# Pooled v of the early pairs by TensorE products, later loads and later product places for the first late pairs

## The chip, the cores and the metric

The kernel runs on one core of one Trainium2 chip. The metric is device time in microseconds, from the runs of the whole program; lower is better. The kernel before takes 948.91 us, the median of three runs (948.26 to 949.22).

## What is computed

A batch of 8 goes through attention and a mixing feed-forward. The attention has two parts: one over sequences pooled by four (a mean of four neighbours of q, k and v), repeated back to full length, and one local part in which each position sees the three neighbours on each side. Their sum x goes into a low-rank mix over positions and a two-layer FFN.

```
B, H, S, D = 8, 8, 576, 64
q_d, k_d, v_d = mean over groups of 4 positions          # 144 positions
out_up    = repeat(softmax(q_d k_d^T / 8) v_d, 4)
out_local = softmax(mask(|i - j| < 4, q k^T / 8)) v
x = out_up + out_local, heads side by side               # 576 x 512 per batch
u = x + (x^T U V)^T                                      # rank 32
out = u + relu(u W1) W2                                  # 512 -> 2048 -> 512
```

## The kernel before, in words

The work is 32 **pairs** of heads, four to a batch, numbered 0 to 31 here. Pairs 0 to 4 (`NE = 5`) take the early path, all others the late path. The early path ends quickly, since TensorE (PE) has nothing else to do until the four pairs of the first batch are finished; the late path gives the local part to GpSimd (POOL) and VectorE (DVE) through DRAM, beside the FFN.

The **FFN** runs per half batch of 288 positions in 16 steps: `ffn1` takes 12 products (L908: high and low parts of u and W1) into a PSUM bank `ps_h`, ScalarE (ACT) makes `hH` from it by ReLU, DVE `hL`, and three steps later `ffn2` takes 12 products (L931) into four accumulators. The 16 blocks of W1 and 16 of W2 are loaded once, as raw 32-bit halves into three shared buffers (`w1r`, `w2r`), and converted (`convert`, L355): ACT makes `upper` (L358), DVE `c` (L361), ACT the high part (L365), and DVE or POOL the low part (L369; DVE for the first eight W1 blocks).

An **early pair** has two strands. `early_global` (L442) pools q and k on POOL (`smq`, `smk`), multiplies them on PE into two banks `ps_s` (L455), takes the row maxima (DVE), the exponentials `E_e` (ACT), transposes them (`ps_t`, L488, copied back by ACT, L491) and multiplies them with the pooled v, `vs_e` (`ps_a`, L500). That `vs_e` is made by POOL in two sums (L459, L461) from `vre`, a load of v of its own (`load_vr`, L591). `local_blocks` (L611) makes scores of 32 positions against 38 keys (`ps_b`, L607), their exponentials `ms_b`, transposes (`ps_bt`, L647) and the products with the windows of v, `vw` (`ps_ba`, L659). `vw` has two buffers that the pairs take in turn (`vw_115` for pairs 0, 2 and 4, `vw_116` for 1 and 3), as have `vs_e` and `E_e`. Both strands meet in `early_mix` (L668: `ps_hu`, `ps_u`), which writes u as `uH` (ACT, L710) and `uL` (DVE).

A **late pair** loads `gq`, `gT` and two `vr`, pools on POOL, multiplies into `ps_b` (L735 and L742, one block of products), copies the local scores out to DRAM (ACT `se`, L760; `s_s`), takes exponentials `E` (L539), transposes (`ps_t`, L553), copies back (L557) and multiplies (`ps_a`, L566).

**The order** of all instructions is set ahead of time by a planner (`Plan.run`, L112). It plays the five engines with assumed durations; on each engine, of the operations that are ready, the one with the smallest priority number is next. Pair p has priorities 10p to 10p + 2, the FFN fills (from 1000 up). So pairs 5 and 6 have 50 to 72. A `margin` (L102) delays the time at which an operation counts as ready: 0.5 us for PE operations of priority 50 to 999 that depend on another engine. A load may not begin in the plan before `at`, 25 us for priorities from 35 up (L276). All loads are issued by SyncE (SP), which keeps its order and stops at a load whose buffer isn't free. PSUM for `ps_s` of pair p and `ps_b` of pair p + 1 is the same two banks.

Of the kernel before, what the change touches and what calls it, by code (L numbers as in the profile page):

```python
# [11 lines left out]
F32 = mybir.dt.float32  # L12
# [58 lines left out]
class Plan:  # L71
# [147 lines left out]
def attn_mix_ffn_kernel(ctx: ExitStack, tc, q, kp, vl_in, qT, kT, v, U, Ub, V, w1, w2_in, mask, band, eye, pool, vw, ident, outT):  # L219
# [221 lines left out]

    def early_global(b, hp, prio, qt, kt, vr):  # L442
        sq = work(True, glo, [128, SD], F32, "smq")
# [8 lines left out]
        def s_mm():  # L452
# [5 lines left out]
        vs = ring([4, D], "vs_e")  # L458
        pool_tt(512, lambda: nc.gpsimd.tensor_tensor(  # L459
            out=vr()[:, :, 0:2 * D], in0=vr()[:, :, 0:2 * D], in1=vr()[:, :, 2 * D:4 * D], op=ALU.add), [vr], [vr], prio, 2.2)  # L460
        pool_tt(256, lambda: nc.gpsimd.tensor_tensor(  # L461
            out=vs()[:QH], in0=vr()[:, :, 0:D], in1=vr()[:, :, D:2 * D], op=ALU.add), [vr], [vs], prio, 2.2)
        E = ring([4, SD], "E_e")
# [18 lines left out]
        for hh in range(2):  # L482
            pt = psum(ps_m, "ps_t", "m:g", 2)

            def t_mm(hh=hh, pt=pt):
                for c in range(2):
                    for a in range(2):
                        nc.tensor.transpose(view(pt, SD)[:, c, a * QH:(a + 1) * QH],  # L488
                                            E()[:QH, 2 * hh + a, c * QH:(c + 1) * QH], ident_sb[:QH, :QH])
            op(PE, 0.44, t_mm, [(E, hh), "ident"], [pt], prio)  # L490
            act(288, lambda hh=hh, pt=pt: nc.scalar.activation(E()[:QH, 2 * hh:2 * hh + 2], view(pt, SD), AF.Copy),  # L491
                [pt], [(E, hh)], prio, 0.12)
        pa = psum(ps_m, "ps_a", "m:g", 2)
        out = lambda: pa()[:QH, :4 * D].rearrange("p (a h d) -> p a h d", a=2, h=2)

        def a_mm():
            for hh in range(2):
                for a in range(2):
                    for c in range(2):
                        nc.tensor.matmul(out()[:, a, hh, :], E()[:, 2 * hh + c, a * QH:(a + 1) * QH],  # L500
                                         vs()[:, 2 * hh + c, :], start=(c == 0), stop=(c == 1))
        op(PE, 1.2, a_mm, ek + [vs], [pa], prio)
        od = work(True, glo, [QH, 2, 2, D], F32, "od")
# [87 lines left out]
    def load_vr(b, h0, prio):  # L591
        t = buf(early_pool, [QH, 4, 4 * D], F32, "vre", None, 2)
        dma(lambda: nc.sync.dma_start(out=t().rearrange("p (h a) x -> p h a x", h=2), in_=v[b, h0:h0 + 2].rearrange(
            "h (a p r) d -> p h a (r d)", a=2, r=4)), [], [t], prio, 480)
        return t

# [359 lines left out]
    def attention(b, pairs=range(HP)):  # L956
        for hp in pairs:
            p = 10.0 * (b * HP + hp)
            if b * HP + hp < NE:
# [104 lines left out]
```

## Time and profile before

One profiled execution took 949.7 us; its span, from the first instruction to the last, is 947.9 us.

| | us |
|---|---|
| median of the runs | 948.91 |
| profiled execution | 949.7 |
| its span | 947.9 |
| first FFN product begins | 65.47 |
| last PE product ends | 943.7 |

A profile row of an engine reads: start, duration, engine, line, operation, output <- inputs, shape, count, and in brackets the idle time ahead of it with what ended it. The row of a group has busy time and mean duration behind the first bar, and the idle time ahead of its members behind the second. Windows give, for a stretch of time, the busy time of every engine, the clock granted to TensorE and the share of the DMA engines' time. A product of floats shows as two records.

### The profile page before, as it was taken

To read this page: it belongs to the slowest core of one execution; us is meant where nothing else is said; L and a number is where in the kernel's file an instruction comes from. 1 tells how busy PE (TensorE), PEld (TensorE's weight loads), DVE (VectorE), ACT (ScalarE), POOL (GpSimd) and SP (SyncE) were. 2 spreads that over 40 slices of the span, in tenths; PEclk is the share of its full clock that TensorE was granted. 3 is DMA by queue.
4 is the path that set the end of the run, shared out by engine and by line. 5 is a ranking of instruction groups with operands and counts; after the bars stand their busy time and mean duration, and the time that the engine had idled before them with its cause. 6 is when DMAs were issued, how large, how long until landed. Compare 5 with 4: busy or idle time off the path is not lost.

```text
span 947.9 us, 26576 instructions
## 1 busy us (share of the span) xinstructions
PE 921.7 (97%) x10805; PEld 903.6 (95%) x10805; DVE 473.9 (50%) x958; ACT 383.8 (40%) x1221; POOL 524.0 (55%) x563
## 2 busy tenths in 40 slices
PE   5799899999999999999999999999999999999998
PEld 4678899999999999999999999999999999999998
DVE  4784755545645444565555555444565544322212
ACT  4687744434443344443344344443443343121111
POOL 5655776675666564775758747565655546021010
PEclk9899899999999999999999999999999999999999
DMA  9977555564454545544565455456444442200000
GB/s 274 300 241 257 170 137 149 132 152 115 127 131 115 123 103 147 138 107 124 138 155 133 119 132 136 109 132 155 115 128 125 120 90 58 64 1 26 6 21 26
DMA packets 215977, 119.19 MB, mean 126 GB/s; under 512 B 168132, under 2 KB 192304, under 8 KB 215856
## 3 DMA queue, kind: packets, MB, share of 16 engines
q1 hardware_dynamic: 215856, 117.51, 48.3%
q8 instruction: 85, 1.39, 0.6%
q14 instruction: 36, 0.29, 0.1%
HBM read 87.37 MB, written 30.09 MB: 124 GB/s over the span
## 4 chain that ended last, share of the span: by engine, by line
PE 87%; DMA 5%; DVE 3%; ACT 3%; issue 1%; SPq 1%; DVEq 0%; ACTq 0%
PE acc L931 38%; PE ps_h L908 37%; PE ps_a L566 3%; PE ps_b L735 2%; PE ps_hu L864 2%; PE ps_t L553 1%; PE ps_b L742 1%; DMA w2r<-in_W 1%; DVE c L361 1%; DMA w1r<-in_W 1%; ACT upper L358 1%; PE ps_u L879 1%; DMA gT<-in_kT 1%; DMA ur<-in_Ub 1%; DMA ur<-in_U 1%
## 5 line engine op out<-in xcount | busy, mean ns | idle before, releaser
L815 POOL TENSOR_TENSOR Pt<-vl,at 128x896 f32<-128x896 f32 (+1 forms) x135 | 219.1, 1689 | 143.3 <-DVE at L798 74.7
L908 PE MATMUL ps_h<-uH,W1H 128*128 128x288 f32 x1024 | 295.0, 288 | 1.0 <-DVE hL L916 0.7
L908 PE MATMUL ps_h<-uL,W1H 128*128 128x288 f32 x1024 | 293.2, 286 | 0.0
L908 PE MATMUL ps_h<-uH,W1L 128*128 128x288 f32 x1024 | 293.0, 286 | 0.0
L916 DVE SCALAR_TENSOR_TENSOR hL<-ps_h,hH 128x288 fp32r<-128x288 f32 x256 | 116.6, 455 | 334.7 <-ACT hH L915 334.3
L915 ACT ACTIVATE hH<-ps_h 128x288 fp32r<-128x288 f32 x256 | 104.7, 409 | 372.4 <-PE ps_h L908 371.4
L931 PE MATMUL acc<-hH,W2a 128*128 128x288 f32 x1024 | 218.7, 292 | 0.0
L908 PEld LDWEIGHTS ps_h<-uH,W1H 128*128 128x128 f32 x1024 | 193.9, 189 | 2.0 <-DVE hL L916 1.0
L908 PEld LDWEIGHTS ps_h<-uL,W1H 128*128 128x128 f32 x1024 | 193.8, 189 | 0.0
L908 PEld LDWEIGHTS ps_h<-uH,W1L 128*128 128x128 f32 x1024 | 193.8, 189 | 0.0
L931 PEld LDWEIGHTS acc<-hH,W2a 128*128 128x128 f32 x1024 | 171.2, 191 | 0.4
L931 PE MATMUL acc<-hL,W2a 128*128 128x288 f32 x512 | 147.6, 288 | 0.0
L820 DVE TENSOR_REDUCE acc<-Pt 128x128 f32<-128x1024 f32 (+1 forms) x135 | 145.3, 1105 | 4.0 <-ACT Pt L809 2.8
L931 PE MATMUL acc<-hH,W2c 128*128 128x288 f32 x512 | 109.9, 291 | 0.0
L931 PE MATMUL acc<-hH,W2b 128*128 128x288 f32 x512 | 106.9, 288 | 0.0
L931 PEld LDWEIGHTS acc<-hL,W2a 128*128 128x128 f32 x512 | 97.9, 191 | 0.0
L856 POOL TENSOR_TENSOR xL<-xL,xH 116x640 fp32r<-116x640 f32 x27 | 41.8, 1547 | 90.1 <-ACT xH L855 83.0
L931 PEld LDWEIGHTS acc<-hH,W2c 128*128 128x128 f32 x512 | 85.2, 189 | 0.3
L931 PEld LDWEIGHTS acc<-hH,W2b 128*128 128x128 f32 x512 | 84.5, 189 | 0.1
L931 PE MATMUL acc<-hL,W2b 128*128 128x288 f32 x256 | 73.2, 286 | 0.0
L931 PE MATMUL acc<-hL,W2c 128*128 128x288 f32 x256 | 73.2, 286 | 0.0
L941 POOL TENSOR_TENSOR o<-uH,uL 128x288 f32<-128x288 f32 x48 | 37.0, 795 | 49.0 <-DMA out_t<-o 43.8
(141 smaller groups left out, 1286.6 us busy)
## 6 DMA issues: line engine op xcount, KB each, us to landing
vl<-in_vl SPq DMA_DIRECT2D x27, 480.0 KB
w1r<-in_W SPq DMA_DIRECT2D x16, 511.8 KB
w2r<-in_W SPq DMA_DIRECT2D x16, 511.8 KB
gT<-in_kT SPq DMA_DIRECT2D x27, 291.0 KB
gq<-in_qT SPq DMA_DIRECT2D x27, 288.0 KB
vr<-in_v SPq DMA_DIRECT2D x54, 144.0 KB
up_s<-od SPq DMA_DIRECT2D x108, 72.0 KB
ul<-up_s SPq DMA_DIRECT2D x27, 288.0 KB
```

Source lines behind the costliest of these rows:

```text
L358: act(n, lambda: nc.scalar.activation(c()[:pp, :n].bitcast(F16).rearrange("p (n two) -> p n two", two=2)[:, :, 1], raw()[:pp, :2 * n].bitc ...
L566: nc.tensor.matmul(out()[:, 2 * hh + a, :], Es[hh]()[:, c, a * QH:(a + 1) * QH], vss[hh]()[:, c, :], start=(c == 0), stop=(c == 1))
L735: nc.tensor.matmul(ps[hh]()[c * QL:(c + 1) * QL, r * KL:(r + 1) * KL], qr()[o, n * QL:(n + 1) * QL], kr()[o, n * QL:n * QL + KL], start=Tr ...
L815: nc.gpsimd.tensor_tensor(out=Pt()[:, :n, :, 0:7].rearrange("p s d o -> p o s d"), in0=win, in1=at()[:, ps, :].rearrange("p s o -> p o s") ...
L820: dve(8.5 * n * D, lambda n=n, ps=ps, Pt=Pt: nc.vector.tensor_reduce(out=acc()[:, ps, :], in_=Pt()[:, :n], axis=AX.X, op=ALU.add), [(Pt, 0 ...
L856: pool_tt(640, lambda: nc.gpsimd.tensor_tensor(out=xL(), in0=xL().bitcast(F32), in1=xH().bitcast(F32), op=ALU.subtract), [xL, xH], [xL], prio)
L864: nc.tensor.matmul(pv(), Ust[:, j, :], xx()[:, :, j, :], start=(i == 0 and j == 0), stop=(i == 1 and j == MJ - 1))
L908: nc.tensor.matmul(ps()[:, :TN], w[:, dc, fs], turns(u()[:, dc, :]), start=(n == 0), stop=(n == 3 * NDC - 1))
L915: last_h[i] = act(TN, lambda: nc.scalar.activation(hH(), ps()[:, :TN], AF.Relu), [ps], [hH], FIRST, 0.05)
L916: dve(TN, lambda: nc.vector.scalar_tensor_tensor(hL(), ps()[:, :TN], 0.0, hH().bitcast(F32), op0=ALU.max, op1=ALU.subtract), [ps, hH], [hL ...
L931: nc.tensor.matmul(ac[e]()[:, :TN], w2(fc, w)[:, es], turns(hx()), start=(fc == 0 and n == 0), stop=(fc == NFC - 1 and n == 2))
L941: pool_tt(TN, lambda e=e, o1=o1: nc.gpsimd.tensor_tensor(out=o1()[:, :TN].bitcast(F32), in0=uH()[:, e, :].bitcast(F32), in1=uL()[:, e, :]. ...
```

## The change

The pooled v of pairs 0 to 4 comes from `vw` instead of a load of its own: its windows start three positions ahead of each block of 32, and a stripe matrix of zeros and ones, appended to `pool_sb` (144 to 200 columns), adds up four rows at a time. 18 blocks times two heads are 36 products per pair, written into free columns of the two `ps_s` banks, and four DVE copies take them to `vs_e`. The load of `vre` and both POOL sums go. Since the sums lie now as 128 + 16 pooled positions instead of 72 + 72, the transposes of E are cut as 128 and 16: one copy stays on ACT (144 columns instead of 288), one of 16 rows goes to DVE.

Three settings move as well. The PE margin for priorities 49 to 69 becomes 2.0. Loads of priority 49 and up may not begin in the plan before 42 us. Low parts of W1 go to POOL from block 4 on instead of 8.

```diff
-MARGIN, MARGIN_FROM = (0.5,0.0,0.0,0.0,0.0), 50
+MARGIN, MARGIN_FROM, FIRST_MARGIN = (0.5, 0.0, 0.0, 0.0, 0.0), 50, 2.0
...
-        o.margin = MARGIN[eng] * (MARGIN_FROM <= prio < 1000 and any(d.eng != eng for d in deps))
+        o.margin = (FIRST_MARGIN if eng == PE and prio < 70 else MARGIN[eng]) * (
+            MARGIN_FROM - 1 <= prio < 1000 and any(d.eng != eng for d in deps))
...
-        return op(SP, issue, fn, r, w, prio, move=0.01 + kb / 390.0, at=AT if prio >= 35 else 0.0, lat=lat + late)
+        return op(SP, issue, fn, r, w, prio, move=0.01 + kb / 390.0, at=42 if prio >= 49 else AT if prio >= 35 else 0.0, lat=lat + late)
...
-        convert(raw, 128, CN, lambda: W1H[:, :, fs], lambda: W1L[:, :, fs], NDC, f"W1_{f}", "c1", prio, rest=DVE if f < 8 else POOL)
+        convert(raw, 128, CN, lambda: W1H[:, :, fs], lambda: W1L[:, :, fs], NDC, f"W1_{f}", "c1", prio, rest=DVE if f < 4 else POOL)
...
-        pool_tt(512, lambda: nc.gpsimd.tensor_tensor(
-            out=vr()[:, :, 0:2 * D], in0=vr()[:, :, 0:2 * D], in1=vr()[:, :, 2 * D:4 * D], op=ALU.add), [vr], [vr], prio, 2.2)
-        pool_tt(256, lambda: nc.gpsimd.tensor_tensor(
-            out=vs()[:QH], in0=vr()[:, :, 0:D], in1=vr()[:, :, D:2 * D], op=ALU.add), [vr], [vs], prio, 2.2)
+        def v_mm():
+            for c in range(4):
+                for g in range((NL - c + 3) // 4):
+                    for hh in range(2):
+                        o = slice(hh * KW, (hh + 1) * KW)
+                        nc.tensor.matmul(ps[hh]()[g % 4 * QL:(g % 4 + 1) * QL, 2 * SD + g // 4 * D:2 * SD + (g // 4 + 1) * D],
+                                         pool_sb[o, 168 - 8 * c:168 - 8 * c + QL], vw_t()[o, 4 * g + c, :],
+                                         start=(c == 0 and g < 4), stop=(c == 3))
+        op(PE, 0.9, v_mm, [vw_t, "pool"], [(p, "v") for p in ps], prio)
+        for hh in range(2):
+            for c, n in enumerate((128, QL)):
+                dve(D, lambda hh=hh, c=c, n=n: nc.vector.tensor_copy(out=vs()[:n, 2 * hh + c, :], in_=ps[hh]()[:n, 2 * SD + c * D:2 * SD + (c + 1) * D]),
+                    [(ps[hh], "v")], [(vs, hh, c)], prio)
...
-            act(288, lambda hh=hh, pt=pt: nc.scalar.activation(E()[:QH, 2 * hh:2 * hh + 2], view(pt, SD), AF.Copy),
-                [pt], [(E, hh)], prio, 0.12)
+            act(SD, lambda hh=hh, pt=pt: nc.scalar.activation(E()[:, 2 * hh], pt()[:, :SD], AF.Copy), [pt], [(E, hh)], prio, 0.12)
+            dve(SD, lambda hh=hh, pt=pt: nc.vector.tensor_copy(
+                out=E()[:SD - 128, 2 * hh + 1], in_=pt()[:SD - 128, SD:2 * SD]), [pt], [(E, hh)], prio)
...
-                od = early_global(b, hp, p, qt, kt, load_vr(b, 2 * hp, p))
+                od = early_global(b, hp, p, qt, kt, vw_t)
```

Because the planner sets the order, it moves in many places. Three of them follow; lines behind the changed ones have moved by up to 12 (L607 is now L613, L908 is L914).

The first is PE at the start of the program, from the scores of pair 0 to the first `ps_a`. In a row stand line, operation, output <- inputs, shape and count; `ps_up` pools U. Before:

```order
L607 MATMUL ps_b<-kd,qt 32x38 x36
L455 MATMUL ps_s<-smk,smq 72x144 x4
L647 MATMUL ps_bt<-ident_sb,ms_b_103 128x128 x5
L488 MATMUL ps_t<-ident_sb,E_e_111 72x72 x4
L386 MATMUL ps_up<-Ublk,pool_sb 72x64 x6
L488 MATMUL ps_t<-ident_sb,E_e_111 72x72 x4
L619 LDWEIGHTS eye_sb
L619 MATMUL ps_b<-band_sb,eye_sb 128x190
L619 LDWEIGHTS eye_sb
L619 MATMUL ps_b<-band_sb,eye_sb 128x190
L607 MATMUL ps_b<-kd,qt 32x38 x36
L500 MATMUL ps_a<-vs_e_107,E_e_111 72x64 x8
```

And now:

```order
L613 MATMUL ps_b<-kd,qt 32x38 x36
L456 MATMUL ps_s<-smk,smq 72x144 x4
L465 MATMUL ps_s<-vw_115,pool_sb 32x64 x36
L387 MATMUL ps_up<-Ublk,pool_sb 72x64 x6
L499 MATMUL ps_t<-ident_sb,E_e_111 128x72 x2
L499 MATMUL ps_t<-ident_sb,E_e_111 16x72 x2
L653 MATMUL ps_bt<-ident_sb,ms_b_103 128x128 x5
L499 MATMUL ps_t<-ident_sb,E_e_111 128x72 x2
L499 MATMUL ps_t<-ident_sb,E_e_111 16x72 x2
L456 MATMUL ps_s<-smk,smq 72x144 x4
L465 MATMUL ps_s<-vw_116,pool_sb 32x64 x36
L512 MATMUL ps_a<-vs_e_107,E_e_111 72x64 x8
```

The products of `vw` and `pool_sb` (L465) of pairs 0 and 1 stand ahead of the transposes and of `ps_a`, and the pooled scores of pair 1 have moved ahead of its local scores.

The second is ACT around the scores of pair 6 (`se`, `E`) and the conversions of the last W2 blocks and of U (`ur`, `Ust`). Before:

```order
L358 ACTIVATE upper_86<-w2r 128x512
L536 ACTIVATE nb<-mx 72x2
L358 ACTIVATE upper_87<-ur 116x160
L539 ACTIVATE E,rs<-ps_b,nb 72x144 x2
L365 ACTIVATE W2b<-c_1912 128x512
L365 ACTIVATE Ust<-cu 116x5x32
L915 ACTIVATE hH<-ps_h 128x288
L536 ACTIVATE nb<-mx 72x2
L539 ACTIVATE E,rs<-ps_b,nb 72x144 x2
```

And now:

```order
L359 ACTIVATE upper_87<-ur 116x160
L366 ACTIVATE W2b<-c_2028 128x512
L921 ACTIVATE hH<-ps_h 128x288
L366 ACTIVATE Ust<-cu 116x5x32
L766 ACTIVATE se<-ps_b 96x114
L766 ACTIVATE se<-ps_b 32x342
L766 ACTIVATE se<-ps_b 96x114
L766 ACTIVATE se<-ps_b 32x342
L548 ACTIVATE nb<-mx 72x2 x2
L551 ACTIVATE E,rs<-ps_b,nb 72x144 x3
L921 ACTIVATE hH<-ps_h 128x288
L551 ACTIVATE E,rs<-ps_b,nb 72x144
```

All conversions now stand ahead of the first copy `se` of pair 6. On PE, between pair 5's transposes and its `ps_a` there are 42 FFN products where there were 24, and between pair 6's scores and its transposes 48 where there were 72.

The third is SP, from the loads of pair 4 on (`qt`, `kd`, `vw_115`) to those of pair 5 (`gq`, `gT`, `vr`, `vl`) and the W1 blocks among them. Before:

```order
L583 DMA qt<-in_qT 128x576
L599 DMA kd<-in_kT 128x582
L583 DMA gq<-in_qT 128x576
L583 DMA gT<-in_kT 128x582
L522 DMA vr<-in_v 72x2x256
L783 DMA vl<-in_vl 128x960
L410 DMA w1r<-in_W 128x2047 x2
L588 DMA vw_115<-in_vw 128x1152
L410 DMA w1r<-in_W 128x2047
```

And now, from the `vw_116` of pair 3:

```order
L600 DMA vw_116<-in_vw 128x1152
L411 DMA w1r<-in_W 128x2047 x3
L600 DMA vw_115<-in_vw 128x1152
L411 DMA w1r<-in_W 128x2047 x3
L595 DMA gq<-in_qT 128x576
L411 DMA w1r<-in_W 128x2047
L595 DMA gT<-in_kT 128x582
L534 DMA vr<-in_v 72x2x256
L789 DMA vl<-in_vl 128x960
L411 DMA w1r<-in_W 128x2047 x3
```

Pair 5's loads have moved behind pair 4's last one. Six blocks of W1 stood ahead of its `gq` and ten behind it; now twelve stand ahead, and the last three behind `vl`.

More of the change, by code (lines that the diff above doesn't have):

```diff
@@ L323, in attn_mix_ffn_kernel @@
     eye_sb = early_pool.tile([128, 128], BF16, name="eye_sb")
-    pool_sb = early_pool.tile([128, 144], F32, name="pool_sb")
+    pool_sb = early_pool.tile([128, 200], F32, name="pool_sb")
     Ublk = early_pool.tile([128, NS, 2 * R], F32, name="Ublk")
@@ L440, in pool_halves, with early_global @@
             out=out(), in0=gh()[..., 0], in1=gh()[..., 1], op=ALU.add), [gh], [out], prio, 1.75)
-    def early_global(b, hp, prio, qt, kt, vr):
+    def early_global(b, hp, prio, qt, kt, vw_t):
         sq = work(True, glo, [128, SD], F32, "smq")
@@ L486, in t_mm @@
                 for c in range(2):
+                    n = (128, SD - 128)[c]
                     for a in range(2):
-                        nc.tensor.transpose(view(pt, SD)[:, c, a * QH:(a + 1) * QH],
-                                            E()[:QH, 2 * hh + a, c * QH:(c + 1) * QH], ident_sb[:QH, :QH])
+                        nc.tensor.transpose(pt()[:n, c * SD + a * QH:c * SD + (a + 1) * QH],
+                                            E()[:QH, 2 * hh + a, c * 128:c * 128 + n], ident_sb[:QH, :QH])
             op(PE, 0.44, t_mm, [(E, hh), "ident"], [pt], prio)
-            act(288, lambda hh=hh, pt=pt: nc.scalar.activation(E()[:QH, 2 * hh:2 * hh + 2], view(pt, SD), AF.Copy),
-                [pt], [(E, hh)], prio, 0.12)
+            act(SD, lambda hh=hh, pt=pt: nc.scalar.activation(E()[:, 2 * hh], pt()[:, :SD], AF.Copy), [pt], [(E, hh)], prio, 0.12)
+            dve(SD, lambda hh=hh, pt=pt: nc.vector.tensor_copy(
+                out=E()[:SD - 128, 2 * hh + 1], in_=pt()[:SD - 128, SD:2 * SD]), [pt], [(E, hh)], prio)
         pa = psum(ps_m, "ps_a", "m:g", 2)
@@ L501, in a_mm @@
                                          vs()[:, 2 * hh + c, :], start=(c == 0), stop=(c == 1))
-        op(PE, 1.2, a_mm, ek + [vs], [pa], prio)
+        op(PE, 1.2, a_mm, ek + [(vs, hh, c) for hh in range(2) for c in range(2)], [pa], prio)
         od = work(True, glo, [QH, 2, 2, D], F32, "od")
@@ L589, in load_vw @@
         return vw_t
[L591 to L595, printed above, removed]
     def load_kd(b, h0, prio):
@@ L1030 @@
     pool = np.arange(128)[:, None] // 4 + 64 == np.arange(144)[None, :]
+    own = np.arange(128)[:, None] % 64 - 3
+    pool = np.concatenate([pool, (own // 4 + 24 == np.arange(56)[None, :]) & (own >= 0) & (own < 32)], axis=1)
     arrays = {
```

## The prediction, made before the result was known

> **What bounds the kernel now.** Read the page's head first, then the windows, one row to a stage.
>
> ```profile
> span 947.9 us, 26576 instructions
> ...
> PE 921.7 (97%) x10805; PEld 903.6 (95%) x10805; DVE 473.9 (50%) x958; ACT 383.8 (40%) x1221; POOL 524.0 (55%) x563
> ```
> ```profile
> 0.00:20.00 20.00, 10.56 (x221) 8.40 (x221) 9.51 (x26) 8.21 (x28) 11.15 (x22) 1.00 0.91 271
> 20.00:34.00 14.00, 11.00 (x263) 8.80 (x263) 7.25 (x17) 8.71 (x33) 8.74 (x12) 0.88 0.94 290
> 34.00:65.00 31.00, 27.50 (x573) 22.58 (x573) 26.90 (x59) 25.38 (x75) 17.29 (x21) 0.94 0.85 270
> 65.00:92.00 27.00, 25.57 (x296) 23.98 (x294) 14.76 (x25) 19.81 (x48) 16.77 (x13) 1.00 0.75 238
> 92.00:125.00 33.00, 29.27 (x310) 28.32 (x309) 23.03 (x39) 19.93 (x54) 24.46 (x25) 0.90 0.61 185
> 125.00:900.00 775.00, 774.03 (x8798) 767.98 (x8797) 382.39 (x775) 296.00 (x970) 442.49 (x469) 1.00 0.47 113
> ```
>
> The columns are window, length, busy time (and instructions) of PE, PEld, DVE, ACT and POOL, then granted clock, DMA share and GB/s. From 125 us on PE idles 1 us in 775: nothing on another engine is worth anything there, and only work put on PE or taken from it counts. All that the change can win or lose lies before: PE idles 9.4, 3.0 and 3.5 us in the first three windows, 1.4 and 3.7 us in the next two. The clock falls to 0.88, 0.94 and 0.90 in three of them. Next, PE's timeline shows where; the bracket is the idle time and what ended it.
>
> ```profile
> 10.99 1.30 PE L647 MATMUL ps_bt<-ident_sb,ms_b 128*128 128x128 f32 x5 [2.79 <-DMA ident_sb<-in_ident]
> ...
> 12.81 0.57 PE L488 MATMUL ps_t<-ident_sb,E_e 72*72 72x72 f32 x3 [0.40 <-ACT E_e L473]
> 13.40 1.70 PE L386 MATMUL ps_up<-Ublk,pool_sb 128*72 128x64 f32 x12
> ...
> 20.28 0.79 PE L659 MATMUL ps_ba<-vw,et 38*32 38x64 f32 x56 [1.12 <-issue]
> ...
> 33.70 0.27 PE L607 MATMUL ps_b<-kd,qt 64*32 64x38 f32 x7 [2.68 <-issue]
> ...
> 34.44 0.85 PE L607 MATMUL ps_b<-kd,qt 64*32 64x38 f32 x72
> ...
> 41.01 1.03 PE L659 MATMUL ps_ba<-vw,et 38*32 38x64 f32 x80
> ...
> 65.47 0.39 PE L908 MATMUL ps_h<-uH,W1H 128*128 128x288 f32 x1 [0.28 <-DVE ob L663]
> ```
> ```profile
> 89.85 0.67 PE L553 MATMUL ps_t<-ident_sb,E 72*72 72x72 f32 x8
> ...
> 94.44 0.73 PE L566 MATMUL ps_a<-vs,E 72*72 72x64 f32 x8 [0.94 <-ACT E L557]
> ...
> 95.96 0.73 PE L566 MATMUL ps_a<-vs,E 72*72 72x64 f32 x8 [0.79 <-ACT E L557]
> ...
> 112.06 0.45 PE L553 MATMUL ps_t<-ident_sb,E 72*72 72x72 f32 x4 [0.46 <-ACT E L539]
> ...
> 114.05 0.69 PE L553 MATMUL ps_t<-ident_sb,E 72*72 72x72 f32 x4 [1.54 <-ACT E L539]
> ```
>
> No wait of PE ends at the pooled v, neither at its load nor at its two sums. The FFN begins at 65.47; pairs 5 and 6 then stop PE four times, 0.94 + 0.79 + 0.46 + 1.54 = 3.73 us, all on ScalarE. The clock rows behind these stops:
>
> ```profile
> 96.00:100.00 4.00, 4.00 (x24) 4.00 (x25) 3.30 (x6) 2.90 (x6) 4.00 (x5) 0.62 0.93 336
> 100.00:104.00 4.00, 4.00 (x118) 3.79 (x117) 3.16 (x5) 1.78 (x5) 2.44 (x2) 0.96 0.45 120
> ...
> 112.00:116.00 4.00, 2.39 (x14) 2.23 (x15) 2.03 (x5) 3.92 (x17) 4.00 (x4) 0.75 0.26 27
> 116.00:120.00 4.00, 4.00 (x29) 4.00 (x28) 2.92 (x5) 1.09 (x3) 4.00 (x4) 0.82 0.03 5
> ```
>
> The missing clock is 4 x (0.38 + 0.04) = 1.7 us behind the first two stops and 4 x (0.25 + 0.18) = 1.7 us behind the second two. So the stops and their clock hold 3.7 + 3.4 = 7.1 us.
>
> **The change, part by part.** *Products for the pooled v.* Five pairs get 36 products each; PE's records count a product of floats twice, so the 72 records of the scores (0.85 us) and the 80 of the local sums (1.03, or 0.93 for 72) are the like: small tiles, four column groups and two row halves in turn. I take 0.9 us, 4.5 us for five.
>
> Pair 0's stand ahead of everything that PE began at 10.99 and wait for `pool_sb`, whose landing no row shows. It was issued after `ident_sb`, which ended the wait at 10.99, and one load of 288 KB less stands ahead (1.1 us at 271 GB/s): not before 9.9. At 13.40 it was there. I take 12.0, so the queue behind starts 12.0 + 0.9 - 11.0 = 1.9 us later and loses its wait of 0.40: +1.5 us, ends -0.2 and +3.3.
>
> The other four cost 3.6 us in windows where PE idles 3.0 + 3.5 us of 45. Nothing assigns them to the gaps: I take 2.6, ends 0 and 3.6.
>
> *Removed.*
>
> ```profile
> L459 POOL TENSOR_TENSOR vre<-vre 72x512 f32<-72x512 f32 x5 | 6.3, 1265 | 8.8 <-DMA vre<-in_v 8.8
> ...
> L461 POOL TENSOR_TENSOR vs_e<-vre 72x256 f32<-72x256 f32 x5 | 3.6, 727 | 3.9 <-PE ps_a L500 3.8
> ```
> ```profile
> vre<-in_v SPq DMA_DIRECT2D x5, 288.0 KB
> ```
> ```profile
> L491 ACT ACTIVATE E_e<-ps_t 72x288 f32<-72x288 f32 x10 | 4.0, 399 | 4.0 <-PE ps_t L488 4.0
> ```
> ```profile
> L504 DVE TENSOR_TENSOR od<-ps_a,ri 72x256 f32<-72x256 f32 x5 | 2.1, 417 | 1.9 <-PE ps_a L500 1.9
> ...
> L639 DVE RECIPROCAL ri_b<-re 128x10 f32<-128x10 f32 x5 | 1.0, 206 | 0.3 <-ACT re L638 0.3
> ```
>
> POOL loses 9.9 us, the load queue 1.44 MB (5.1 us at 280 GB/s), ACT about a third of each of ten copies (1.2 us). DVE gains 20 copies of 64 columns and 10 of 144, between 206 and 417 ns each: about 0.23 and 0.29, 7.5 us in all, and loses four subtractions of W1. Its windows have 6.8 and 4.1 us idle between 20 and 65 us, so they hide, if they don't stand ahead of a score reduction; then they are in the late end below. POOL takes those four over, in time that it has gained. The loads for pair 5 also leave the queue in front of pair 4's (the third place shown in the section on the change). This relief can return at most the 6.5 us that PE idles from 20 to 65, and at least nothing, since two of these waits, 1.12 and 2.68, ended at nothing that the trace names. I take about half, -3.1 us. Up to the FFN's start: 1.5 + 2.6 - 3.1 = **+1.0 us**, bounds -6.7 and +6.9.
>
> *The later places of pairs 5 and 6.* An FFN product takes 1.47 / 12 = 0.1225 us:
>
> ```profile
> 117.63 1.47 PE ps_h L908 x12
> ```
> ```profile
> 93.07 0.77 ACT L358 ACTIVATE upper<-w2r 128x512 f16<-128x512 bf16 x1 [3.23 <-DMA w2r<-in_W]
> ...
> 95.52 0.39 ACT L557 ACTIVATE E<-ps_t 72x288 f32<-72x288 f32 x1
> ...
> 110.94 0.39 ACT L358 ACTIVATE upper<-ur 116x160 f16<-116x160 bf16 x1 [0.93 <-DMA ur<-in_U]
> ```
> ```profile
> 113.17 0.83 ACT E L539 x4
> ```
> ```profile
> 80.79 1.48 ACT L760 ACTIVATE se<-ps_b 96x114 f32<-96x114 f32 x4
> ```
>
> Pair 5's transposes ended at 90.5 and ScalarE's second copy at 95.9, behind a conversion that waited 3.23 us for W2. Between transposes and `ps_a` stood 24 FFN products (2.9 us), now 42 (5.1 us); the first half of `ps_a` takes 0.7 us more, so the second copy is needed 5.8 us after the transposes and took 5.4. Both waits and their 1.7 us of clock go: -3.4. Pair 6 waited for its exponentials behind the conversion of U (110.94). U's conversion now stands before the copies out of the scores, and no conversion stands among the exponentials. But between scores and transposes there are 48 FFN products (5.9 us) where there were 72 (8.8). Four copies (1.5 us), four exponentials (two with their sums took 0.83, so 1.7) and two scalings and a ReLU copy, none longer than the 0.39 of a copy of E (1.2), make 4.4 us and the semaphores: it just fits unless U or W2 lands late. I count a quarter of its 3.7 us as won, 0.9. Together **-4.3 us**, bounds -7.1 and +1.0.
>
> The clock gate can be weighed here: after stops of 0.94 and 0.79 us the clock reads 0.62. The Trainium skill, "TensorE: Matmul & The Clock Gate", Part 1, has the half clock come only after an idle window of about 3.4 us. By that rule stops this short would cost no clock and the gain would be 1.7 + 0.5 instead of 3.4 + 0.9, a time of 947.7; the row differs from it, and decides.
>
> *Sum.* +1.0 - 4.3 = -3.3 us. The profiled execution took 949.7 us, 1.8 above its span of 947.9; 949.7 - 3.3 = 946.4. The median of the runs is 0.8 below that execution: **945.6 us**.
>
> **Rivals.** *Weights late, slower.* Before pair 3's last `uH` ScalarE now converts 16 blocks of W1 and one of W2, where it converted 13 and wrote 12 high parts; the last three W1 loads, all ahead of `uH` now, stand right behind 1.2 MB for pair 5.
>
> ```profile
> 61.53 0.63 ACT L365 ACTIVATE W1H<-c 128x512 fp32r<-128x512 f32 x1
> ...
> 62.44 0.77 ACT L358 ACTIVATE upper<-w1r 128x512 f16<-128x512 bf16 x1
> ...
> 63.08 0.39 ACT L710 ACTIVATE uH<-ps_u 128x288 fp32r<-128x288 f32 x1
> ```
>
> Four more conversions of 0.77 and as many high parts of 0.63 are 5.6 us on an engine that keeps its order and had 5.6 us idle of 31, and 1.2 MB is 4.4 us of loading. It decides if the sixteenth W1 block lands after about 62 us, since `uH` ran at 63.08. If the FFN starts 6.5 us later, +6.5 - 4.3 = +2.2; with pair 6's gain gone too, +3.1: 951 to 952 us. For it: DVE and ACT are the fullest there (26.9 and 25.4 of 31). Against it: the loads begin earlier, with 1.44 MB less to carry.
>
> *Moved, not won, within 0.2%.* The relief is worth little, the early part costs 2 to 4 us, and only pair 5's 3.4 come back: -1.4 to +0.6, 947.5 to 949.5. For it: no wait of PE ended at the pooled v, so 4.5 us of new products buy nothing by themselves. Against it: the gaps of pair 5 have a clear cause and a clear cover.
>
> *Products that don't overlap, slower.* If the 36 products run one by one like the transposes (four in 0.45 us, row 112.06), they take 4 us a pair, 20 in all, 15.5 more than counted: 961 us. Against it: the 72 records at 34.44, laid out in the same way, take 12 ns each. The Trainium skill, "TensorE: Matmul & The Clock Gate", section "Back-to-back issue gap", has starts never closer than about 25 ns, which by that page makes 1.8 us a pair and a time of about 950; the row is below that floor.
>
> **Chances.** Forecast 0.56, moved 0.24, weights late 0.15, no overlap 0.05. A measurement of this kernel tells about 0.2% (1.9 us) from no change, so faster is below 947.0 and slower above 950.8: 0.56, 0.24, 0.20. The range takes most of the early bounds with the late gain, 941, and the late weights, 952; about 0.06 is left on either side.
>
> **What would show it.** The v products as one block of about 0.9 us a pair; the first of them ended by a load near 12 us; the FFN's first product at 65 to 68 us; no wait in front of pair 5's `ps_a`, a small one at most in front of pair 6's transposes, and a clock of 1.0 behind both; PE's busy time up by some 2 to 5 us and still no idle time after 125 us. I am wrong if the FFN starts after 70, if ScalarE stands at a W1 or U load for over 2 us with PE waiting behind it, or if PE starts to wait after 125 us because pairs 5 to 7 come too late for the second batch.

## The result, and the profile after

The changed kernel takes longer:

| | before | changed |
|---|---|---|
| median of 5 runs each, us | 948.91 | 956.07 (953.30 to 958.95) |
| ratio, 95% interval | | 1.0070 (1.0045 to 1.0095) |
| profiled execution, us (span) | 949.70 (947.9) | 956.07 (954.3) |
| first FFN product of TensorE, us | 65.47 | 73.58 |
| from there to the end of the span, us | 882.4 | 880.7 |

A later set of runs, with 23 of before, gave 956.52 and 1.0085 (1.0065 to 1.0104). The forecast was 945.6 with a range up to 952: the sign was wrong, and the time lies outside the range. The whole loss stands ahead of the FFN.

The head of the changed kernel's page and its windows, with the columns of the prediction's rows (window, length, busy time and instructions of PE, PEld, DVE, ACT, POOL, then clock, DMA share, GB/s):

```profile
span 954.3 us, 27312 instructions
...
PE 923.5 (97%) x11165; PEld 905.5 (95%) x11165; DVE 481.9 (51%) x984; ACT 385.5 (40%) x1221; POOL 521.5 (55%) x557
```
```profile
0.00:20.00 20.00, 11.13 (x349) 9.07 (x350) 10.39 (x34) 9.00 (x34) 9.37 (x22) 1.00 0.78 278
20.00:34.00 14.00, 10.34 (x212) 8.63 (x211) 8.99 (x25) 8.49 (x25) 2.18 (x4) 0.88 0.54 183
34.00:65.00 31.00, 25.25 (x809) 20.49 (x808) 22.70 (x64) 23.23 (x76) 18.38 (x17) 1.00 0.79 261
65.00:92.00 27.00, 23.48 (x271) 21.40 (x265) 14.25 (x24) 13.81 (x30) 14.27 (x13) 0.87 0.53 173
92.00:125.00 33.00, 29.08 (x323) 27.70 (x321) 21.34 (x30) 23.44 (x59) 24.03 (x20) 1.00 0.67 203
125.00:900.00 775.00, 774.05 (x8805) 768.25 (x8806) 392.36 (x786) 300.91 (x987) 450.15 (x479) 1.00 0.48 115
```

From 125 us on nothing has changed. In 92 to 125 the clock is back at 1.00 from 0.90, as forecast. In 34 to 65 PE issues 809 products where it issued 573, and idles 5.75 us where it idled 3.50. Its timeline shows what those waits are:

```profile
18.52 0.99 PE L665 MATMUL ps_ba<-vw,et 38*32 38x64 f32 x74
21.21 0.31 PE L665 MATMUL ps_ba<-vw,et 38*32 38x64 f32 x6 [1.70 <-issue]
...
23.36 0.54 PE L613 MATMUL ps_b<-kd,qt 64*32 64x38 f32 x37
26.35 0.51 PE L613 MATMUL ps_b<-kd,qt 64*32 64x38 f32 x35 [2.45 <-issue]
...
39.07 0.33 PE L653 MATMUL ps_bt<-ident_sb,ms_b 128*128 128x128 f32 x1 [1.10 <-issue]
...
49.44 0.27 PE L613 MATMUL ps_b<-kd,qt 64*32 64x38 f32 x6 [2.50 <-issue]
...
58.15 0.80 PE L465 MATMUL ps_s<-vw,pool_sb 64*32 64x64 f32 x35
59.92 0.63 PE L465 MATMUL ps_s<-vw,pool_sb 64*32 64x64 f32 x37 [0.97 <-issue]
...
65.57 0.41 PE L665 MATMUL ps_ba<-vw,et 38*32 38x64 f32 x19 [0.51 <-issue]
...
73.58 0.59 PE L914 MATMUL ps_h<-uH,W1H 128*128 128x288 f32 x1
```

Six stops "issue", that is, stops that end at nothing the trace names, sum to 9.23 us; before had two, 1.12 + 2.68 = 3.80. Most of them cut through the middle of a block of equal products (74 and 6, 37 and 35) whose operands are the same two tiles, so an operand is unlikely to be what was waited for. All other idle time ahead of the FFN is the same: 12.5 us against 12.35. PE's busy time there is 51.85 us against 49.32. So of the FFN's 8.1 us of delay, 5.4 are these stops and 2.5 busy time.

Where do they stand? The windows from 0 to just ahead of each stop count what PE had issued; the numbers behind x in the first two groups are its products and its weight loads. Changed kernel, then before:

```profile
0.00:21.20 21.20, 11.13 (x349) 9.07 (x350) 10.88 (x34) 10.20 (x37) 9.37 (x22) 1.00 0.77 269
0.00:26.34 26.34, 13.82 (x476) 11.18 (x476) 14.50 (x45) 13.16 (x45) 9.37 (x22) 1.00 0.80 283
0.00:39.06 39.06, 25.38 (x730) 20.96 (x730) 24.27 (x73) 21.79 (x73) 13.80 (x30) 0.96 0.71 248
0.00:49.43 49.43, 33.24 (x985) 27.13 (x985) 30.32 (x89) 29.46 (x96) 21.19 (x34) 0.97 0.74 251
0.00:59.91 59.91, 42.76 (x1238) 34.77 (x1239) 39.59 (x112) 36.62 (x117) 26.95 (x39) 0.97 0.73 249
0.00:65.56 65.56, 46.78 (x1366) 38.19 (x1367) 42.65 (x123) 41.07 (x132) 30.48 (x44) 0.97 0.73 247
```
```profile
0.00:20.27 20.27, 10.56 (x221) 8.40 (x221) 9.51 (x26) 8.21 (x28) 11.42 (x23) 1.00 0.91 270
0.00:33.69 33.69, 21.27 (x475) 16.95 (x476) 16.75 (x43) 16.91 (x61) 19.58 (x33) 0.95 0.92 279
```

The two counts of a row add up to 699, 952, 1460, 1970, 2477 and 2733, and 442 and 951: always 442 plus a multiple of 254, within 7 records, whatever line stands there. The queues in section 3 of the two pages, changed kernel first, say what comes in pieces of that size:

```profile
q8 instruction: 88, 1.44, 0.6%
q14 instruction: 36, 0.29, 0.1%
```
```profile
q8 instruction: 85, 1.39, 0.6%
q14 instruction: 36, 0.29, 0.1%
```

The columns are packets and MB. A packet of q8 has 16.4 KB. PE's records of a whole run, products and weight loads together, are 2 x 11165 = 22330 and 2 x 10805 = 21610: 253.8 and 254.2 for each packet of q8, while q14 has as many packets in both. In all fourteen profiles PE's records over 254 give the packets of q8 within one. So the reading is: PE's instructions come by DMA in blocks of about 254, and PE stops where it has used up a block before the next is there. In the changed kernel, PE went on after these stops at 26.35, 39.07, 49.44 and 59.92 us, each two blocks after the one before: a block every 6.4, 5.2 and 5.2 us. In 34 to 65 us its 1617 records in 31 us would need one every 4.9. During four of the six stops the DMA engines are full or nearly so (DMA share is the last but one column). In that of 1.70 us it was 0.41, and in that of 0.51 us nothing moved, so full engines are not the whole reason why a block comes late; the rest stays open.

```profile
23.90:26.30 2.40, 0.00 (x0) 0.00 (x0) 1.27 (x4) 0.80 (x2) 0.00 (x0) 1.00 0.99 318
...
38.00:39.00 1.00, 0.00 (x0) 0.00 (x0) 1.00 (x4) 0.85 (x5) 1.00 (x3) 1.00 1.03 375
...
47.00:49.40 2.40, 0.00 (x0) 0.00 (x0) 0.49 (x2) 0.79 (x2) 2.40 (x2) 1.00 0.87 284
...
59.00:60.00 1.00, 0.07 (x9) 0.07 (x13) 0.50 (x2) 0.00 (x0) 0.00 (x0) 1.00 1.11 259
```

### The profile page after: what moved, and what is told of

Read it like the earlier page. It is cut to its first block, busy times and chain, and to the rows that moved or that the text cites. A ratio compares the mean times of both kernels' runs of the same rounds, so it can differ in the third digit from the quotient of the medians.

```text
span 954.3 us, 27312 instructions
## 1 busy us (share of the span) xinstructions
PE 923.5 (97%) x11165; PEld 905.5 (95%) x11165; DVE 481.9 (51%) x984; ACT 385.5 (40%) x1221; POOL 521.5 (55%) x557
## 4 chain that ended last, share of the span: by engine, by line
PE 90%; DMA 2%; DVE 2%; ACT 2%; issue 2%; POOL 1%; SPq 0%; DVEq 0%; POOLq 0%; ACTq 0%
PE acc L937 38%; PE ps_h L914 38%; PE ps_a L578 3%; PE ps_b L741 2%; PE ps_hu L870 2%; PE ps_t L565 1%; PE ps_b L748 1%; DVE c L362 1%; PE ps_u L885 1%; POOL W1L L370 1%; DMA w2r<-in_W 1%; DMA gT<-in_kT 1%; DMA vraw<-in_V 1%; ACT upper L359 1%; PE ps_s L465 0%
## 5 line engine op out<-in xcount | busy, mean ns | idle before, releaser
L914 PE MATMUL ps_h<-uH,W1H 128*128 128x288 f32 x1024 | 296.1, 289 | 2.7 <-DVE hL L922 2.7
L914 PE MATMUL ps_h<-uL,W1H 128*128 128x288 f32 x1024 | 294.0, 287 | 0.0
L914 PE MATMUL ps_h<-uH,W1L 128*128 128x288 f32 x1024 | 294.0, 287 | 0.0
L914 PEld LDWEIGHTS ps_h<-uH,W1H 128*128 128x128 f32 x1024 | 194.7, 190 | 3.9 <-DVE hL L922 3.3
L914 PEld LDWEIGHTS ps_h<-uL,W1H 128*128 128x128 f32 x1024 | 194.6, 190 | 0.0
L914 PEld LDWEIGHTS ps_h<-uH,W1L 128*128 128x128 f32 x1024 | 194.6, 190 | 0.0
L893 POOL TENSOR_TENSOR uL<-xT,uH 128x288 fp32r<-128x288 f32 x54 | 42.0, 799 | 69.4 <-ACT uH L891 69.4
```

The costliest lines, as they stand in the source:

```text
L893: pool_tt(TN, lambda uH=uH, uL=uL, uf=uf: nc.gpsimd.tensor_tensor(out=uL()[:, hp, :], in0=uf(), in1=uH()[:, hp, :].bitcast(F32), op=ALU.su ...
L914: nc.tensor.matmul(ps()[:, :TN], w[:, dc, fs], turns(u()[:, dc, :]), start=(n == 0), stop=(n == 3 * NDC - 1))
```

## The experiments

The theory is **supply**, the blocks of instructions above. By it a product costs its records, not only its time, and loads that are taken away pay because blocks come sooner. There are two rivals. **Time**: only the products' own time on PE and the waits between engines count. **Settings**: the four numbers changed beside the v products (margin, loads from 42, W1's low parts of blocks 4 to 7 on GpSimd) cost the time. Three sets ran, each beside before; ratios are to that before, with 95% intervals. "Stops" are those put down to issue ahead of the FFN in the profiled execution.

| kernel | median us | ratio | stops, us | FFN starts |
|---|---|---|---|---|
| before (set 1 / 2 / 3) | 948.94 / 948.51 / 948.15 | | 3.80 | 65.47 |
| 1 dense products | 957.65 | 1.0077 (1.0047 to 1.0108) | 4.23 | 76.17 |
| 1 large products | 956.07 | 1.0089 (1.0056 to 1.0121) | 6.19 | 70.70 |
| 1 settings alone | 948.76 | 0.9997 (0.9975 to 1.0019) | 4.16 | 67.58 |
| 1 v change alone | 952.42 | 1.0040 (1.0021 to 1.0059) | 7.85 | 73.21 |
| 2 changed kernel again | 956.52 | 1.0085 (1.0065 to 1.0104) | 9.11 | 75.06 |
| 2 v as 6 large products | 947.74 | 0.9996 (0.9981 to 1.0011) | 0.26 | 65.27 |
| 2 v by 10 products of 36 | 946.90 | 0.9983 (0.9969 to 0.9996) | 0.20 | 66.01 |
| 2 margin of before | 955.61 | 1.0071 (1.0053 to 1.0088) | 6.37 | 73.32 |
| 3 before, small v loads | 942.60 | 0.9946 (0.9924 to 0.9968) | 0.74 | 61.79 |
| 3 loads of before | 952.61 | 1.0056 (1.0037 to 1.0076) | 8.55 | 70.45 |
| 3 W1 of before | 960.18 | 1.0135 (1.0114 to 1.0156) | 7.65 | 72.32 |
| 3 v as 12 large products | 950.86 | 1.0022 (1.0006 to 1.0037) | 0.50 | 70.58 |

**Set 1: products added to before, and the change in two halves.** Dense products, in `s_mm` of before:

```diff
                                     start=True, stop=True)
+            for n in range(18):
+                for hh, o in enumerate(heads):
+                    nc.tensor.matmul(ps[hh]()[n % 4 * QL:(n % 4 + 1) * QL, 2 * SD:2 * SD + D],
+                                     sq()[o, :QL], sk()[o, :D], start=True, stop=True)
```

> The kernel of before, in which each early pair's block of pooled score products (L455) issues 36 more products of the size of the v products (K 64, 32 rows out, 64 columns), whose results nothing reads; pooled v stays on GpSimd and every setting is that of before. The theory of instruction supply (TensorE stands, for nothing that the trace names, where it has used up a block of some 254 records before the next has come): 144 more TensorE records a pair, 720 in all, as in the change; the stops put down to issue before the FFN grow from 3.8 us to 7 to 10 us, each at a multiple of about 254 records, PE's busy time grows by 4 to 6 us, and the FFN starts 7 to 11 us later: 954 to 960 us. The rival, that only the products' own time and the waits between engines cost: the stops put down to issue stay at 3 to 5 us, the time rises by no more than the products' 4 to 6 us: 949 to 954 us.

Large products, at the same place:

```diff
+            for n in range(4):
+                for hh, o in enumerate(heads):
+                    nc.tensor.matmul(ps[hh]()[:QH, 2 * SD:3 * SD],
+                                     sq()[o, n % 2 * QH:(n % 2 + 1) * QH], sk()[o], start=True, stop=True)
```

> The kernel of before, in which each early pair's block of pooled score products issues 8 more products of its own size (72 rows out, 144 columns), unread: about the same TensorE time as the 36 small ones of the other kernel of this set (some 1 us a pair), but 32 records a pair in place of 144. The theory of instruction supply: stops put down to issue stay at 3 to 5.5 us, time 949 to 953 us, at least 3 us below the kernel with small products. The rival, that TensorE's time and the waits between engines cost: within 1.5 us of the kernel with small products.

This pair missed. The dense kernel's time came as the theory had it, the stops did not, and the large products cost nearly as much (956.07, outside the theory's 949 to 953, and within 1.6 us of the other). The groups of the added products, dense and large:

```profile
0.00:75.00 75.00, 6.32 (x360) 0.86 0.76 238
```
```profile
0.00:75.00 75.00, 7.01 (x80) 0.89 0.81 256
```

(busy time of these products alone in the first 75 us, then clock, DMA share and GB/s.) The large ones took 7.0 us and cost 7.1; the dense ones took 6.3 and cost 8.7. By these medians added PE time counts about one for one in the kernel of before, and what is left for the records is too small beside the intervals. The large kernel's median is also a poor measure: its ten runs fall apart into six of 953.1 to 956.4 us, of which the profile is one, and four of 962.0 to 964.8; by the ratios it is the dearer of the two. And by windows of 1 us up to 75 us, PE loses 9.1 us to the lower clock in the dense kernel, 8.3 in the large one and 3.4 in before. This pair decides nothing between supply and time. Nor is the sum of the stops a measure of supply: in the dense kernel PE ran at half clock from 47 to 60 us, below the pace of the blocks, and had no need to stop. Where it did stop, the grid holds: 1208, 1462, 1717 and 1973 records in the one, 442, 1206 and 1968 in the other.

The settings alone, on before:

```diff
-MARGIN, MARGIN_FROM = (0.5,0.0,0.0,0.0,0.0), 50
+MARGIN, MARGIN_FROM, FIRST_MARGIN = (0.5, 0.0, 0.0, 0.0, 0.0), 50, 2.0
...
-        return op(SP, issue, fn, r, w, prio, move=0.01 + kb / 390.0, at=AT if prio >= 35 else 0.0, lat=lat + late)
+        return op(SP, issue, fn, r, w, prio, move=0.01 + kb / 390.0, at=42 if prio >= 49 else AT if prio >= 35 else 0.0, lat=lat + late)
...
-        convert(raw, 128, CN, lambda: W1H[:, :, fs], lambda: W1L[:, :, fs], NDC, f"W1_{f}", "c1", prio, rest=DVE if f < 8 else POOL)
+        convert(raw, 128, CN, lambda: W1H[:, :, fs], lambda: W1L[:, :, fs], NDC, f"W1_{f}", "c1", prio, rest=DVE if f < 4 else POOL)
```

> The kernel of before with the change's four settings alone (the margin of 2.0 for TensorE's priorities 49 to 69 and the wider range, loads of late pairs from 42, three to seven W1 blocks more to GpSimd), pooled v still on GpSimd. The theory of instruction supply: no more small products, so the settings do not make the loss; stops put down to issue stay at 3 to 5.5 us and the time is 944 to 949.5 us. The rival, that the settings (the weights' late conversion and loads) cost the time and the FFN's late start: 952 to 957 us.

The v change alone is the changed kernel with these lines turned back.

> The change with before's settings: pooled v on TensorE, margins, load times and W1's engine as before. The theory of instruction supply: stops put down to issue of 7 to 11 us before the FFN, and a time of 953 to 959 us, near the whole change. The rival, that the settings cost: 946 to 950 us.

The settings alone move nothing (0.9997); the v change alone loses 0.4% and has the long stops (7.85 us, at 699, 952, 1460 and 1969 records). Its time lies just below the theory's range. The two do not add to the whole change's 0.7 to 0.85%.

**Set 2: inside the changed kernel.** The runs on the v products keep its order and its waits. The changed kernel again:

> The changed kernel itself, run beside the kernels of this set so that they are compared on one chip. The first set gave 1.0040 for the v change alone and 0.9997 for the settings alone; if the two add, this is 1.002 to 1.006 (950.5 to 954.5 us); if they work against each other, 1.006 to 1.009 again (954.5 to 957.5 us).

It repeated, so halves of 0.4% and nothing make 0.85%: they work against each other. The large products in place of the v products:

```diff
         def v_mm():
-            for c in range(4):
-                for g in range((NL - c + 3) // 4):
-                    for hh in range(2):
-                        o = slice(hh * KW, (hh + 1) * KW)
-                        nc.tensor.matmul(ps[hh]()[g % 4 * QL:(g % 4 + 1) * QL, 2 * SD + g // 4 * D:2 * SD + (g // 4 + 1) * D],
-                                         pool_sb[o, 168 - 8 * c:168 - 8 * c + QL], vw_t()[o, 4 * g + c, :],
-                                         start=(c == 0 and g < 4), stop=(c == 3))
+            for c in range(3):
+                for hh in range(2):
+                    o = slice(hh * KW, (hh + 1) * KW)
+                    nc.tensor.matmul(ps[hh]()[:, 2 * SD:2 * SD + 2 * D], pool_sb[o, 0:128],
+                                     vw_t()[o, 2 * c:2 * c + 2, :], start=(c == 0), stop=(c == 2))
```

> The changed kernel in which the 36 v products of each early pair are replaced by 6 products of 128 rows out and 128 columns (pooled v is then not the pooled v: no sum over the right rows): some 0.8 to 1.1 us of TensorE time a pair as before, 24 records in place of 144. The theory of instruction supply: the stops put down to issue fall from 9.2 us to 3 to 6 us, and the time by 2.5 to 5 us against the changed kernel, to 951 to 953.5 us. The rival, that the products' time on TensorE alone counts: within 1.5 us of the changed kernel, and where stops put down to issue go, waits for other engines take their place.

This is the run that decides. The same PE time, 600 records fewer, and 8.8 us gone (956.52 to 947.74), more than the theory had asked. The stops fall by as much, from 9.11 to 0.26 us. The time of these products alone in the first 75 us, of the changed kernel and of this one, and then the only stop that this one has left:

```profile
0.00:75.00 75.00, 6.31 (x360) 0.96 0.73 245
```
```profile
0.00:75.00 75.00, 6.72 (x60) 0.95 0.76 255
```
```profile
22.43 0.59 PE L611 MATMUL ps_b<-kd,qt 64*32 64x38 f32 x43 [0.26 <-issue]
```

6.72 us of products against 6.31: the rival "time" would have it slower. As an estimate, at the pace of 5.2 us a block, 600 records are 2.4 blocks or 12 us of supply, of which 8.8 us show.

Ten v products of 36:

```diff
-            for c in range(4):
+            for c in range(1):
...
-                                         start=(c == 0 and g < 4), stop=(c == 3))
+                                         start=(c == 0 and g < 4), stop=(g != 0))
```

> The changed kernel with 10 of the 36 v products of each early pair (the first of the four groups; three quarters of the sum over the rows are left out), all waits and the order as they are: 104 fewer records and some 0.65 us less TensorE time a pair. The theory that the products' time on TensorE counts, about one for one: 2 to 4.5 us below the changed kernel, 951.5 to 954 us. The theory of instruction supply on top of it: 5 to 8 us below, 948 to 951 us. A third, that neither counts and the waits for the window load, for VectorE's copies and for the weights do: within 1.5 us of the changed kernel.

It is 9.6 us below the changed kernel, more than either theory had asked. Against the six large products it saves 3.8 us more of PE time (2.88 against 6.72) and only 0.8 us of the run: once the blocks come in time, PE's own time counts for less than one for one here.

The margin of before:

```diff
-MARGIN, MARGIN_FROM, FIRST_MARGIN = (0.5, 0.0, 0.0, 0.0, 0.0), 50, 2.0
+MARGIN, MARGIN_FROM, FIRST_MARGIN = (0.5, 0.0, 0.0, 0.0, 0.0), 50, 0.5
...
-            MARGIN_FROM - 1 <= prio < 1000 and any(d.eng != eng for d in deps))
+            MARGIN_FROM <= prio < 1000 and any(d.eng != eng for d in deps))
```

> The changed kernel with the margin of before (0.5 from 50, no 2.0 for TensorE's early priorities); loads from 42 and W1 on GpSimd from block 4 stay. If the margin is what makes the whole change dearer than the v change alone (early pairs' products put off, so that the FFN and the late pairs start later): 951.5 to 954 us. If it is the weights on GpSimd or the loads, or if there is nothing to explain: within 1.5 us of the changed kernel.

The time is 955.61 us, within 1 us of the changed kernel: the margin is not it.

**Set 3: the loads, the two settings left, and PE time without records.** The kernel of before with a quarter of each v load:

```diff
-            out=vr()[:, :, 0:2 * D], in0=vr()[:, :, 0:2 * D], in1=vr()[:, :, 2 * D:4 * D], op=ALU.add), [vr], [vr], prio, 2.2)
+            out=vr()[:, :, D:3 * D].rearrange("p c (t d) -> p c t d", t=2), in0=vr()[:, :, 0:D].unsqueeze(2).broadcast_to([QH, 4, 2, D]),
+            in1=vr()[:, :, 0:D].unsqueeze(2).broadcast_to([QH, 4, 2, D]), op=ALU.add), [vr], [vr], prio, 2.2)
...
-            out=vs()[:QH], in0=vr()[:, :, 0:D], in1=vr()[:, :, D:2 * D], op=ALU.add), [vr], [vs], prio, 2.2)
+            out=vs()[:QH], in0=vr()[:, :, D:2 * D], in1=vr()[:, :, 2 * D:3 * D], op=ALU.add), [vr], [vs], prio, 2.2)
...
-        dma(lambda: nc.sync.dma_start(out=t().rearrange("p (h a) x -> p h a x", h=2), in_=v[b, h0:h0 + 2].rearrange(
-            "h (a p r) d -> p h a (r d)", a=2, r=4)), [], [t], prio, 480)
+        dma(lambda: nc.sync.dma_start(out=t()[:, :, 0:D].rearrange("p (h a) x -> p h a x", h=2), in_=v[b, h0:h0 + 2].rearrange(
+            "h (a p r) d -> p h a (r d)", a=2, r=4)[:, :, :, 0:D]), [], [t], prio, 480)
```

> The kernel of before with a quarter of the bytes in each early pair's load of v rows (one of four rows; GpSimd adds that row to itself, so three quarters of the sum over rows are left out); every operation, wait and engine else as before. The theory that these loads slow TensorE's instruction blocks, so that taking them away is a real relief: the stops put down to issue fall from 3.8 us to under 2 us and the time to 944 to 947 us. The rival, that the relief of the change was never there: within 1 us of before, the stops at 3 us or more.

The time is 942.60 us, 5.5 us below before and below what was expected. GpSimd's two sums stay where they were and add up the one row that is loaded. The one stop left, and the count ahead of it:

```profile
18.09 0.79 PE L660 MATMUL ps_ba<-vw,et 38*32 38x64 f32 x56 [0.74 <-issue]
```
```profile
0.00:18.08 18.08, 9.87 (x221) 7.68 (x221) 9.12 (x26) 7.97 (x27) 10.56 (x22) 1.00 0.87 283
```

It stands at 442 records again. At 951, where before stopped for 2.68 us, there is no stop now. In the profiles the FFN starts 3.7 us earlier than in before: 3.1 of it are the stops, and the wait for `ident_sb` is 1.2 us shorter; other waits give the rest back.

The changed kernel with `at=AT if prio >= 35 else 0.0`, as before:

> The changed kernel with the load times of before (no loads held back to 42). If the later loads make the whole change dearer than the v change alone (952.4 us against 956.5 us): 951.5 to 954 us. If not: within 1.5 us of the changed kernel, 955 to 958 us.

The time is 952.61 us, in the range expected if the later loads matter: below the changed kernel by 3.9 us by the medians and 2.8 by the ratios. But the two kernels ran in different sets and their intervals overlap (up to 1.0076 and from 1.0065). So it is likely, and not shown, that the later loads make the settings cost on top of the v change, though the settings alone cost nothing. The stops are much the same (8.55 us). The profile of the changed kernel loses more to the lower clock than this one (4.8 us of PE's time by windows of 1 us up to 130 us, against 1.7): from 72 to 78 us its clock is 0.50, behind a wait of PE for `stk` of 2.27 us, which is 0.61 us here. In the second profile of the changed kernel it is a stop of 2.07 us that stands ahead of its half clock from 62 to 72 us, so the way from the loads to the time stays open.

The changed kernel with `rest=DVE if f < 8 else POOL`, as before:

> The changed kernel with W1's low parts of blocks 4 to 7 on VectorE as before. If their place on GpSimd makes the whole change dearer than the v change alone: 951.5 to 954 us. If not: within 1.5 us of the changed kernel, 955 to 958 us.

It came out as neither: with W1 back on VectorE the kernel is 3.7 us (by the ratios 4.8) worse than the changed one. Its trace has a wait that no other has, after 125 us:

```profile
PE ps_u L885 <- DVE stk L875: 3.9, 1, 3.9
```

(what PE waited for: total, times, longest.) So moving these four subtractions to GpSimd was a gain. That it comes through this wait is only read from one trace.

Twelve large products:

```diff
-            for c in range(3):
+            for c in (0, 1, 2, 0, 1, 2):
```

> The changed kernel with 12 products of 128 rows out and 128 columns for each early pair in place of its 36 v products (pooled v is not the sum over the right rows): 1.7 us of TensorE time a pair, about twice that of the v products, in 48 records against 144. The theory of instruction supply: at least 3 us below the changed kernel in spite of its longer products, 948 to 953.5 us, with stops put down to issue below 3 us. The rival, that TensorE's time counts one for one: 4 us above the kernel with 6 large products and more, 952 to 957 us; and if only TensorE's time counted, 4 us above the changed kernel, 960 us.

The time is 950.86 us: the products take 11.25 us, 4.9 more than in the changed kernel, and the run is 5.7 us faster (1.0022 against 1.0085). Against the six large ones, 4.5 us of PE time cost 3.1.

All 46 stops put down to issue in the fourteen profiles stand at 442 plus a multiple of 254 records, within 7. That the stops are PE running out of a block is read from that grid and from the number of the packets; the arrival of a block itself is not in the trace.

## Why the prediction was wrong, point by point

- **The failed step** is the early part's +1.0 us; the FFN started 8.1 us later (9.6 in the second profile), 5.4 by stops and 2.5 by PE's busy time. The prediction had the two stops of 1.12 and 2.68 us in hand and used them as a floor: a relief that might return nothing, "since two of these waits, 1.12 and 2.68, ended at nothing that the trace names". It took them for a fixed loss. By the grid they were the supply of instructions, which the change asks 720 records more of. The large products show what 600 of these records are worth: 8.8 us, with the stops gone (9.11 to 0.26 us).
- **The products' own time** was priced at 0.9 us a pair; the blocks took 0.98 to 1.49 us, 6.3 in all against 4.5, all at a granted clock of 1.00. As time this was 1.8 us too low. The error was that a product was given a duration and no place in the instruction stream.
- **Pair 0 behind `pool_sb`** was taken as +1.5 us. Its products began at 10.83, where 12.0 was taken, and `ps_up` behind them at 12.26, where it had stood at 13.40: no loss there.

```profile
10.83 1.49 PE L465 MATMUL ps_s<-vw,pool_sb 64*32 64x64 f32 x72 [2.57 <-DVE cv L362]
12.26 1.70 PE L387 MATMUL ps_up<-Ublk,pool_sb 128*72 128x64 f32 x12
```

- **The relief** of -3.1 us was real and too small: three quarters of the loads' bytes alone are worth 5.5 us in before. In its profile it comes mostly through the blocks of instructions (3.1 of the 3.7 us by which the FFN starts earlier); GpSimd's 9.9 us did not have to go for it. Relief and PE time cancel: with the records gone, the whole change stands at 0.9996.
- **The late part**, -4.3 us: from the FFN's start on, the changed kernel needs 1.7 us less (3.3 in its second profile). Pair 5's two stops at `ps_a` are gone and the clock is full, as forecast; but stops as long took their place. In 92 to 125 us PE idles 3.92 us, against 3.73 before:

```profile
107.55 0.39 PE L914 MATMUL ps_h<-uH,W1H 128*128 128x288 f32 x1 [0.85 <-DVE hL L922]
113.41 0.39 PE L914 MATMUL ps_h<-uH,W1H 128*128 128x288 f32 x1 [1.56 <-DVE hL L922]
116.77 0.44 PE L748 MATMUL ps_b<-smk,smq 64*32 64x144 f32 x9 [0.90 <-DVE od L582]
```

  Here half of the mechanism was right: of the -4.3, some 2.1 were clock and 2.2 stops. The clock gave more, 3.4 us in 92 to 125, and the stops gave nothing, since they moved from ScalarE to VectorE. What takes the gain down to 1.7 us is the start: up to 78 us the FFN's first products run at a clock of 0.50, some 2.6 us lost, where the second profile starts its FFN at full clock. No experiment took this apart further.
- **"Weights late"** gave the FFN's late start and the sign, with 951 to 952 us, by ScalarE standing at W1's loads. No load ends ScalarE's two long waits from 60 us to there: one ends at PE, the other at VectorE. But that other one is a step of W1's conversion, with PE behind it, as that rival had it: VectorE's `c` takes 2.38 us (its neighbours took 0.67 and 1.23), ScalarE waits 2.47 us for it and writes `stk` only then, and PE waits 2.27 us for `stk`. Why `c` took so long was not tried.

```profile
60.61 0.38 ACT L483 ACTIVATE E_e<-ps_s,nb 72x144 f32<-72x144 f32 x1 [2.23 <-PE ps_s L465]
...
69.46 0.63 ACT L366 ACTIVATE W1H<-c 128x512 fp32r<-128x512 f32 x1 [2.47 <-DVE c L362]
70.00 0.25 ACT L687 ACTIVATE stk<-ps_hu 64x128 fp32r<-64x128 f32 x1
```
```profile
67.05 2.38 DVE L362 SCALAR_TENSOR_TENSOR c<-w1r,upper 128x512 int32<-128x512 int32 x1
```
```profile
70.89 0.40 PE L709 MATMUL ps_u<-Vst,stk 128*128 128x288 f32 x1 [2.27 <-DVE stk L688]
```

  This alone does not make the loss: all idle time ahead of the FFN but the stops is the same as before (12.5 us against 12.35); in the second profile PE does not wait for `stk` and the FFN starts later still; and the kernel with 12 large products has the wait too (2.57 us) and is 5.7 us faster. Taking W1 off GpSimd made things worse. The later loads bear this rival out at most in part (2.8 to 3.9 us).

- **"Products that don't overlap"**: they overlap, 72 records in 0.98 us, 14 ns each, near the 12 ns of the prediction's row of the scores. The Trainium skill, "TensorE: Matmul & The Clock Gate", "Back-to-back issue gap", has a floor of some 25 ns for the isolated gap between products; these, laid out over column groups and row halves, lie below it.

## What to carry to other kernels

Count the instructions that a change adds to a stage, not only their time: where an engine works through hundreds of short ones while loads keep the DMA engines busy, their supply can be the bound. A stop that ends at nothing, in the middle of a block of equal instructions, is not noise: count the records up to each such stop, in two kernels, and see whether the counts fall on one grid. Where they do, fewer and larger products, or fewer bytes loaded in that stage, pay more than their own time.

## What the runs showed of the hardware that was not expected

- PE stops on a grid of about 254 records, and the instruction queue has a packet of 16.4 KB for every 254 records of PE. Between 26 and 60 us a block came every 5.2 to 6.4 us, some 40 to 49 records a us. From 125 us on PE needs 17611 records in 775 us, 23 a us, and stops for none.
- A stop can cost more than itself: behind that of 2.45 us the clock fell to half, though PE was busy throughout the 4 us shown. Behind that of 1.70 us it stayed at 1.00.

```profile
28.00:30.00 2.00, 2.00 (x10) 1.67 (x10) 0.47 (x3) 0.67 (x3) 1.04 (x3) 0.50 0.02 7
30.00:32.00 2.00, 2.00 (x12) 1.64 (x10) 1.71 (x4) 1.45 (x4) 0.07 (x1) 0.74 0.00 0
```

- The runs of one kernel spread by some 9 us (before, 943.83 to 952.65 in 21 runs); stops and half clock differ between two profiles of the changed kernel too (9.23 and 9.11 us of stops, 4.8 and 7.8 us lost to the lower clock). With 12 runs beside 23 of before, the interval of a ratio was still 0.15% (1.4 us) to either side.
